# Gate and up stage in 15 pieces of 512 to 560 tokens instead of 16 of 512

## Chip, cores and metric

The kernel runs on one core of one Trainium2 chip. The metric is the device time of one execution in microseconds (us). Before the change the median of three runs is 2451.41 us (2451.37 to 2451.5).

## What is computed

`x` has shape (2, 1, 4096, 640): two sequences of 4096 tokens, 640 features each, 8192 tokens in all.

```python
g = sigmoid((x * gate_w).sum(-1, keepdims=True))
a = irfft2(mlp(rfft2(x)))        # a two-layer complex MLP in 4 blocks of 160, with ReLU and soft threshold
b = (gelu(x @ w_gate) * (x @ w_up)) @ w_down      # 640 -> 1728 -> 640
out = g * a + (1 - g) * b
```

## The kernel before

Three stages follow each other, and each fills TensorE (PE).

**Gate and up stage** (0 to about 1354 us). It makes `gelu(x @ w_gate) * (x @ w_up)`, called h, and writes it to DRAM (`hD`). The work is tiled by pieces of 512 tokens (16 of them, called tp) and by tiles of 128 of the 1728 columns (t = 0 to 13). A pair (x @ gate tile, x @ up tile) is a 2x2 block product over two halves of 256 tokens and two halves of the features, done with seven products by a scheme of sums (Strassen and Winograd): `quad` (L590). Each fp32 operand is split into a high and a low part (`high`, L285, on ScalarE, ACT; `low`, L288, on VectorE, DVE), and each product is hi·hi + hi·lo + lo·hi, so three matmuls (`prod`, L561; issued by `run`, L569, the matmul itself in L572). Weights are the stationary operand, 128 x 128; the tokens are the moving one, 256 columns. Every matmul loads its own weights.

The loop is over `keys` (L1500): group 0 has tiles 0 to 3, group 1 tiles 4 to 7, group 2 tiles 8 to 13; within a group, over the pieces. A quad is 54 matmuls. Piece 0 of group 0 goes through `plain` (L746), 60 matmuls a tile. For the pieces 3 to 12 (`FIRST`, `LAST`) of groups 0 and 1, called deep, one of the seven products is itself done by such a scheme over two pieces and two tiles: a quad is 48 matmuls there, and `deep_parts` (L692) adds 21 per two pieces and two tiles. Tile 13 is `mixed` (L772), 30 matmuls a piece in group 2.

Beside it run the first steps of the Fourier transform (`a_step`, L821): 64 rows of x, four matmuls of 320 columns each, with a stationary table `F1`, loaded on GpSimd's (POOL's) queue by `f1_load` (L791), five tables a load.

**Spectral stage** (to about 1768 us): `fwd2`, `mlp1`, `mlp2`, `inv1`. **Last stage** (to the end): `inv2` and `down` (L1402), the product with w_down, 32 steps; h is read back by `h_load` (L1318) and the split weights by `wd_load` (L1268).

The order is written out by hand: `spread` puts a step at a slot (seven slots in a quad, `hook`) of a piece, `at` after a tile, `fin` after a step of the spectral stage. `x_prep` (L468) makes the sums and splits of the next piece, or loads them from `xD` if an earlier group has made them. Each engine runs its instructions in this order, and SyncE's (SP's) queue issues most DMAs, in order too.

SBUF is divided into rings of buffers: `big` (L240) 18 buffers of 5120 bytes a partition, `mid` 14 of 4096, `small` 18, `tiny` 15. Weights take `big`, tokens (`xo`) take `mid`.

```python
def big(shape, dt=F32, name="big"):
    return pool.tile(shape, dt, name=name, tag="big", bufs=18)
```

Of the kernel before, what the change touches and what calls it, by code (L numbers as in the profile page):

```python
# [15 lines left out]
P = 128  # L16
# [10 lines left out]
FIRST, LAST = 3, 13  # L27

# [129 lines left out]

def _layouts(a):
# [10 lines left out]
    def apart(a, n):  # L170
# [51 lines left out]
def spectral_mix_kernel(ctx: ExitStack, tc: tile.TileContext, a):  # L222
# [15 lines left out]
    gap = []  # L238

    def big(shape, dt=F32, name="big"):  # L240
        return pool.tile(shape, dt, name=name, tag="big", bufs=18)

    def mid(shape, dt=F32, name="mid"):
        if not gap:
            gap.extend([tiny([P, 1], name="gap"), pool.tile([P, 112], F32, name="gap", tag="gap", bufs=1)])
            for t in gap:
                nc.gpsimd.memset(t, 0.0)
        return pool.tile(shape, dt, name=name, tag="mid", bufs=14)
# [21 lines left out]
    xD = [dram.tile([P, 4, 1024], F32, name=f"xD_{t}") for t in range(16)]  # L270
# [3 lines left out]
    xA = {t: dram.tile([P, 3584], F32, name=f"xA_{t}") for t in range(FIRST, LAST, 2)}  # L274
# [6 lines left out]
    gs = consts.tile([P, 2, 3, 32], F32, name="gs")  # L281
# [47 lines left out]
    def w_prep(t, plain=False):  # L329
# [17 lines left out]
        def st0():  # L347
            if not plain:
                gate_high()
            GR[t] = o["r"][0]  # L350
            if t < NPAIR:
                g, u = o["r"]
                x = small([P, 4, P], name="wt")
                s1, e, s4 = o["s"] = x[:, 0:2], tiny([P, 2, P], name="wt"), x[:, 2:4]
                s23 = o["s23"] = small([P, 4, P], name="wt")
                nc.vector.tensor_add(s1, u[:, 0:2], u[:, 2:4])
                nc.vector.tensor_sub(s23[:, 0:2], s1, g[:, 0:2])
# [12 lines left out]
        def st3():  # L370
            g, u = o["r"]
            e = o["s"][1]
            w2 = o["w2"] = big([P, 5, 2, P], F32R, name="w2")
            high(w2[:, 0:4, 0], o["s23"])
            nc.vector.tensor_sub(e[:, 0], u[:, 4], g[:, 4])
            nc.vector.tensor_scalar(e[:, 1], u[:, 4], -1.0, None, op0=OP.mult)

        def st4():
# [4 lines left out]
            high(w2[:, 4, 0], o["s"][1][:, 0])  # L383
            low(w2[:, 0:4, 1], o["s23"], w2[:, 0:4, 0])

        def st5():
# [4 lines left out]
            high(w1[:, 4, 0], o["s"][1][:, 1])  # L391
            low(w1[:, 0:2, 1], o["s"][0], w1[:, 0:2, 0])
            low(w2[:, 4, 1], o["s"][1][:, 0], w2[:, 4, 0])

        def st6():
# [5 lines left out]
            low(w1[:, 4, 1], o["s"][1][:, 1], w1[:, 4, 0])  # L401
# [66 lines left out]
    def x_prep(key, k, eng=nc.vector):  # L468

        name = XNAMES[k]  # L470
        kept = int(name[1]) - 1 if name in ("t1", "t2", "t3", "t4") else None

        def src():
            d = XT[key]
            if not made(key) and kept is not None:
                m = mid([P, 2, 512], F32R, name="xo")
# [3 lines left out]
            for n, p, q in (("t1", "b12", "b11"), ("t2", "b22", "t1"), ("t3", "b22", "b12"), ("t4", "b21", "t2")):  # L480
                if n not in d and (n == name or (n, name) == ("t1", "t2")):
                    d[n] = small([P, 512], name="xd")
                    nc.vector.tensor_sub(d[n], d[p], d[q])
            if name == "t5":
                d[name] = small([P, 256], name="xd")
                nc.vector.tensor_sub(d[name], d["k4"][:, :256], d["k4"][:, 256:])
            return d[name]

        def hi(copy=high):
            if not made(key) and kept is not None:  # L490
                return
            if name == "t5":
                if not T5:
                    T5.append(mid([P, 2, 2, 256], F32R, name="xo"))
                t = [T5[0][:, keys.index(key) % 2, h] for h in range(2)]
            else:
                m = mid([P, 2, 512], F32R, name="xo")
# [16 lines left out]
    def x_deep(gr, tp):  # L514
# [30 lines left out]
        def sums(k):  # L545
            def f():
                p, q = XT[0, tp]["b21"], XT[0, tp + 1]["b21"]
                a_, b_ = slice(0, 256), slice(256, 512)
                if not k:
                    x = o["x"] = [small([P, 512], name="xd") for i in range(2)]  # L550
# [25 lines left out]
    def h_store(tp, t, h):  # L576
        st(dr(hD, 4 * tp * P * 14 * P + t * P, [[14 * P, P], [P * 14 * P, 4], [1, P]]),
           h.rearrange("p (t n) -> p t n", t=4))

    def x_of(o, *names):  # L580

        tiles = []
        for n in names:
            n, q = n if isinstance(n, tuple) else (n, None)
            h, l = o[n]
            for k in ((0,) if n == "t5" else (0, 1) if q is None else (q,)):
                tiles.append((h[:, 256 * k:256 * k + 256], l[:, 256 * k:256 * k + 256]))
# [4 lines left out]
    def quad(key, t, hook):  # L592
# [3 lines left out]
        half = lambda: bank()[:, :256]  # L596
        T = lambda n: tiny([P, 256], name=n)
# [8 lines left out]
        if ahead_:  # L606
            if t % 2 == 0:
                PB[t] = big([P, 5, 256], name="pb")
            p1, u2 = (PB[t - t % 2][:, 2 * (t % 2) + k] for k in range(2))
        elif dp and t % 2 == 0:  # L610
            p1 = PB[t][:, 4]
# [17 lines left out]
        h = small([P, 512], name="h") if dp and not ahead_ else None  # L629
        if h is not None:  # L630
            u2 = h[:, :256]
# [20 lines left out]
        def half3():  # L652
            run(X, prod(w["s4"], x_of(o, "b22")), first=False)
            v["h"] = small([P, 512], name="h") if not dp else h
            v["h2"] = T("h2") if ahead_ else v["h"][:, 256:]
            gelu(v["h2"], X)

        def half4():
# [5 lines left out]
            elif not dp:  # L664
                nc.vector.tensor_mul(v["h"][:, :256], u2, p1)
# [21 lines left out]
    def half_store(tp, t, q, h):  # L687
        st(dr(hD, (4 * tp + 2 * q) * P * 14 * P + t * P, [[14 * P, P], [P * 14 * P, 2], [1, P]]),
           h.rearrange("p (t n) -> p t n", t=2))

    def deep_parts(gr, tp, t):
# [80 lines left out]
    def mixed(key):  # L772
# [3 lines left out]
        pm = bank()  # L776
        for q, (x0, x1) in enumerate((("b11", "b21"), ("b12", "b22"))):
            run(pm[:, 256 * q:256 * q + 256], prod(ws, x_of(o, x0, x1, ("k4", q))))
        s, h = small([P, 512], name="gelu"), small([P, 512], name="h")
        nc.gpsimd.memset(h[64:], 0.0)  # L780
        nc.scalar.activation(s[:64], pm[:64], AF.Gelu_apprx_tanh)
        nc.scalar.activation(h[:64], pm[64:], AF.Copy)
# [33 lines left out]
    def a_step(b, n2, h):  # L816
        xs = XS.pop((b, n2, h))
        m = n2 if n2 < 16 else 32 - n2
        f = F1[m // 5][:, m % 5]
# [13 lines left out]
    def gates(b):  # L833
        nc.scalar.activation(gs[:, b, 0], G[:, b], AF.Sigmoid)
        nc.vector.tensor_scalar(gs[:, b, 1], gs[:, b, 0], -1.0, 1.0, op0=OP.mult, op1=OP.add)
        nc.vector.tensor_scalar(gs[:, b, 2], gs[:, b, 0], -1.0, None, op0=OP.mult)
# [425 lines left out]
    def wd_load(j, part):  # L1262
# [23 lines left out]
        if part in (2, 5):  # L1286
            x = mid([P, 1024], F32R, name="wx")
            later.append(lambda: go(x[:, :960], wdf[j], 13, 10, 3))
            for k, n in enumerate(("t1", "b21", "t4")):
                put(n, 0, x[:, 320 * k:320 * k + 320])  # L1290
        elif part == 3:
            x = mid([P, 1024], F32R, name="wx")
            n = 3 if j < 6 else 1
            go(x[:, :320 * n], wdl, 7, j, n)
            for k in range(n):
                WM.setdefault(j + k, {}).setdefault("b22", [None, None])[1] = x[:, 320 * k:320 * k + 320]
            if j == 6:
# [506 lines left out]
```

## Time and profile before

| | us |
|---|---|
| median of three runs | 2451.41 |
| the profiled execution | 2451.55 |
| its span, first to last instruction | 2449.8 |
| outside the span | 1.75 |

In the span PE is busy for 2436.6 us (99%), the weight loads (PEld, beside PE) 99%, DVE 81%, ACT 62%, POOL 6%. The granted clock of PE is full in all slices. The DMA engines are busy for about 0.6 of the span.

How to read it: a matmul's record lasts longer than its share of the engine, since matmuls overlap in the pipeline (a mean of 275 ns each, 11196 of them, 1297.9 us busy together). So what a matmul costs is the distance from its start to the next one's; in a window in which PE never stops that is (length of the window + one record's duration) / matmuls counted, since the count takes in those that began just before it.

### The profile page before, as it was taken

How to read it: one execution, taken by the hardware profiler on the slowest of the kernel's cores; microseconds unless marked ns; L12 is line 12 of the kernel's file. 1: busy time of each engine (PE TensorE's matmuls, PEld its weight loads, DVE VectorE, ACT ScalarE, POOL GpSimd, SP SyncE). 2: the span in 40 equal slices, each digit the busy share in tenths (PEclk: the TensorE clock that was granted, in tenths of full speed). 3: DMA queues.
4: the chain of work that ended last, by engine and by line, in shares of the span. 5: the costliest groups of instructions: out<-in, count | busy, mean ns of one | idle time of the engine just before them, and what ended most of it. 6: DMA issues, size and time to landing. Idle time of an engine off the chain costs nothing.

```text
span 2449.8 us, 54273 instructions
## 1 busy us (share of the span) xinstructions
PE 2436.6 (99%) x20243; PEld 2428.4 (99%) x20243; DVE 1989.7 (81%) x4416; ACT 1506.8 (62%) x3565; POOL 150.2 (6%) x218
## 2 busy tenths in 40 slices
PE   9999999999999999999999999999999999999999
PEld 9999999999999999999999999999999999999999
DVE  7777787877777878777766888888898988888887
ACT  5555556666665666666555788888755555555554
POOL 0111100000000000000002211111100000000000
PEclk9999999999999999999999999999999999999999
DMA  6666667677778677777768455557864444444443
GB/s 210 209 230 217 240 208 239 213 263 240 259 231 257 206 252 253 223 246 237 234 212 260 131 160 163 161 159 235 296 211 148 151 151 168 160 162 159 155 143 105
DMA packets 351421, 499.49 MB, mean 204 GB/s; under 512 B 26028, under 2 KB 223276, under 8 KB 351156
## 3 DMA queue, kind: packets, MB, share of 16 engines
q1 hardware_dynamic: 333684, 445.02, 56.2%
q0 software_dynamic: 17472, 51.00, 5.8%
q8 instruction: 159, 2.61, 0.4%
q14 instruction: 106, 0.87, 0.1%
HBM read 307.10 MB, written 188.81 MB: 202 GB/s over the span
## 4 chain that ended last, share of the span: by engine, by line
PE 93%; DMA 2%; DVE 2%; ACT 1%; issue 1%; POOL 0%; SPq 0%; ACTq 0%; DVEq 0%; POOLq 0%
PE bank L572 73%; PE bank L307 13%; PE bank L993 3%; PE bank L704 2%; PE bank L827 1%; PE bank L1079 1%; PE bank L1080 1%; DMA xraw<-in_xT_dram 0%; DMA s<-scr 0%; DMA xo<-xD 0%; DMA scr<-is 0%; DVE w L288 0%; DMA xr<-in_x_dram 0%; DMA sc<-scr 0%; PE bank L1081 0%
## 5 line engine op out<-in xcount | busy, mean ns | idle before, releaser
L572 PE MATMUL bank<-xo,w 128*128 128x256 f32 x11196 | 1297.9, 275 | 3.9 <-DVE u L650 3.1
L572 PEld LDWEIGHTS bank<-xo,w 128*128 128x128 f32 x11196 | 1276.2, 192 | 6.4 <-DVE u L650 4.1
L572 PE MATMUL bank<-wx,ho 128*128 128x320 f32 x4608 | 631.7, 299 | 0.7 <-ACT bank L1429 0.5
L572 PEld LDWEIGHTS bank<-wx,ho 128*128 128x128 f32 x4608 | 627.7, 189 | 1.2 <-ACT bank L1429 0.8
L598 ACT ACTIVATE u<-bank 128x256 f32<-128x256 f32 x328 | 125.4, 382 | 169.8 <-PE bank L572 161.3
L288 DVE TENSOR_TENSOR ho<-hraw,ho 128x640 fp32r<-128x640 f32 (+3 forms) x384 | 194.4, 541 | 23.8 <-ACT ho L285 21.8
L285 ACT ACTIVATE ho<-hraw 128x640 fp32r<-128x640 f32 x320 | 165.9, 571 | 45.6 <-issue 39.4
L288 DVE TENSOR_TENSOR xs<-xr,xs 64x640 fp32r<-64x640 f32 x128 | 104.9, 820 | 69.8 <-ACT xs L285 67.5
L288 DVE TENSOR_TENSOR xo<-xraw,xo 128x512 fp32r<-128x512 f32 x194 | 133.1, 686 | 15.6 <-ACT xo L285 14.2
L650 DVE TENSOR_TENSOR u<-bank,u 128x256 f32<-128x256 f32 x204 | 85.7, 420 | 73.6 <-ACT u L598 72.2
L307 PE MATMUL bank<-wm,h 128*128 128x320 f32 (+1 forms) x792 | 129.7, 300 | 0.5 <-DVE h L1057 0.5
L829 DVE TENSOR_TENSOR as<-bank,as 64x320 f32<-64x320 f32 x256 | 113.7, 482 | 19.5 <-ACT as L828 17.4
L285 ACT ACTIVATE xo<-xraw 128x512 fp32r<-128x512 f32 x194 | 121.6, 627 | 6.7 <-DMA xraw<-in_xT_dram 5.5
L598 ACT ACTIVATE p<-bank 128x256 f32<-128x256 f32 x144 | 55.3, 384 | 107.0 <-DVE h L661 55.6
L307 PEld LDWEIGHTS bank<-wm,h 128*128 128x128 f32 (+1 forms) x792 | 111.8, 186 | 1.9 <-DVE h L1057 0.7
L828 ACT ACTIVATE as<-bank 64x320 f32<-64x320 f32 x256 | 96.8, 426 | 20.9 <-PE bank L827 15.8
L1429 ACT ACTIVATE bank<-bank 128x320 f32<-128x320 f32 x31 | 13.1, 422 | 156.1 <-PE bank L572 150.9
L1423 DVE SCALAR_TENSOR_TENSOR uu<-bank,gs,uu 128x320 f32<-128x320 f32 x191 | 101.8, 547 | 8.2 <-PE bank L572 4.7
L285 ACT ACTIVATE xs<-xr 64x640 fp32r<-64x640 f32 x128 | 93.8, 733 | 21.5 <-DMA xr<-in_x_dram 19.7
L599 ACT ACTIVATE h<-bank 128x256 f32<-128x256 f32 x204 | 77.9, 382 | 32.2 <-PE bank L572 30.4
L1396 DVE SCALAR_TENSOR_TENSOR uu<-bank,gs,uu 128x320 f32<-128x320 f32 x120 | 57.9, 544 | 48.7 <-ACT uu L1395 46.7
L661 DVE TENSOR_TENSOR h<-h,u 128x256 f32<-128x256 f32 x204 | 84.7, 415 | 0.0
(191 smaller groups left out, 3503.1 us busy)
## 6 DMA issues: line engine op xcount, KB each, us to landing
xo<-xD SPq DMA_DIRECT2D x124, 512.0 KB
xraw<-in_xT_dram SPq DMA_DIRECT2D x215, 256.0 KB
hD<-h SPq DMA_DIRECT2D x184, 256.0 KB
hraw<-hD SPq DMA_DIRECT2D x128, 320.0 KB
xD<-xo POOLq DMA_DIRECT2D x64, 512.0 KB, 3.3
sc<-scr SPq DMA_DIRECT2D x65, 320.0 KB
xr<-in_x_dram SPq DMA_DIRECT2D x64, 320.0 KB
scr<-as SPq DMA_DIRECT2D x64, 320.0 KB
```

Of the source, the lines that this page charges most:

```text
L285: nc.scalar.activation(dst, src, AF.Copy, scale=scale)
L288: eng.tensor_sub(dst, src, hi.bitcast(F32))
L307: nc.tensor.matmul(dst, l, by_two(r), start=i == 0, stop=i == len(ops) - 1)
L572: nc.tensor.matmul(dst, l, by_two(r), start=first and i == 0, stop=i == len(ops) - 1, skip_group_check=True)
L598: copy = lambda d, s_: nc.scalar.activation(d, s_, AF.Copy)
L599: gelu = lambda d, s_: nc.scalar.activation(d, s_, AF.Gelu_apprx_tanh)
L650: nc.vector.tensor_add(u4, C, u4)
L661: nc.vector.tensor_mul(v["h2"], v["h2"], v["u4"])
L828: nc.scalar.activation(stg[hi, cs], pa[lo, :320], AF.Copy)
L829: nc.vector.tensor_add(stg[hi, cs], pa[hi, :320], stg[hi, cs])
L993: nc.tensor.matmul(pz.rearrange("p (r e k f) -> p k r e f", r=2, e=2, k=4)[:, kp], SC[b, c, kp][:, o:o + P], ft.rearrange("p (r e f) -> p ...
L1423: nc.vector.scalar_tensor_tensor(dst, x, g, dst, op0=OP.mult, op1=OP.add)
```

## The change

The 8192 tokens are cut into 15 pieces: one of 512 (piece 0), ten of 544 (the deep ones), four of 560 (pieces 1, 2, 13, 14). A half has 256, 272 or 280 tokens, and that is the width of the moving operand.

`big` and `mid` become one ring of 29 buffers of 5120 bytes; `mid = big`. The table `F1` gets a ring of its own with a single buffer of one table; it is loaded 17 times instead of 4. h lies in DRAM as `[128, 14, 8192]` (partition, tile, token) and not by blocks of 128 tokens; a store of h is one run per partition, and a load takes seven runs of 128 tokens per partition. Several preparations stand at later slots, the sigmoid of the gate moves into the spectral stage, and the loads of w_down's weights are cut and ordered differently.

```diff
+KEYS = 15
+def half_of(t):
+    return 256 if t == 0 else 272 if FIRST <= t < LAST else 280
+def first_of(t):
+    return sum(2 * half_of(k) for k in range(t))
...
     def big(shape, dt=F32, name="big"):
-        return pool.tile(shape, dt, name=name, tag="big", bufs=18)
...
-        return pool.tile(shape, dt, name=name, tag="mid", bufs=14)
+        return pool.tile(shape, dt, name=name, tag="big", bufs=29)
+    mid = big
...
-    hD = dram.tile([64, P, 14 * P], F32, name="hD")
+    hD = dram.tile([P, 14, 2 * N], F32, name="hD")
...
     def h_store(tp, t, h):
-        st(dr(hD, 4 * tp * P * 14 * P + t * P, [[14 * P, P], [P * 14 * P, 4], [1, P]]),
-           h.rearrange("p (t n) -> p t n", t=4))
+        st(hD[:, t, first_of(tp):first_of(tp + 1)], h)
...
+        N = half_of(key[1])
-        half = lambda: bank()[:, :256]
-        T = lambda n: tiny([P, 256], name=n)
+        half = lambda: bank()[:, :N]
+        T = lambda n: tiny([P, N], name=n)
...
     def f1_load(q):
-        m = min(5, 17 - 5 * q)
-        F1[q] = big([P, 5, 2, P], F32R, name="f1")
-        nc.gpsimd.dma_start(F1[q][:, :m], a["f1"][:, 5 * q:5 * q + m])
+        F1[q] = pool.tile([P, 2, P], F32R, name="f1", tag="f1", bufs=1)
+        nc.gpsimd.dma_start(F1[q], a["f1"][:, q])
...
-        if k in (0, 18, 38, 58):
-            back(i, sp[0] - 12, lambda q=(k + 2) // 20: f1_load(q))
+        if k % 4 == 2 or not k:
+            back(i, sp[0] - (0 if k else 8), lambda q=(k + 2) // 4: f1_load(q))
...
-            for k, s in enumerate((5, 8, 11, 14, 16, 18, z + 1, z + 4, z + 6) if gr < 2 else
-                                  (6, 9, 13, 17, 21, z + 1, z + 2, z + 3, z + 3, z + 5)):
+            for k, s in enumerate(((5, 8, 11, z - 1, z + 1, 18, z + 3, z + 4, z + 6),
+                                   (5, 8, z - 3, z, z - 2, 18, z + 1, z + 5, z + 4),
+                                   (6, 9, z - 3, z + 3, z - 2, z + 1, z + 1, z + 5, z + 4, z + 6))[gr]):
...
         if part in (2, 5):
-            x = mid([P, 1024], F32R, name="wx")
-            later.append(lambda: go(x[:, :960], wdf[j], 13, 10, 3))
+            x = mid([P, 1280], F32R, name="wx")
+            def both():
+                go(x[:, 960:], wdl, 7, j, 1)
+                go(x[:, :960], wdf[j], 13, 10, 3)
+            later.append(both)
...
-    keys = [(gr, tp) for gr in range(3) for tp in ([1, 2, 0, *range(3, 16)] if gr == 1 else range(16))]
+    keys = [(gr, tp) for gr in range(3) for tp in ([1, 2, 0, *range(3, KEYS)] if gr == 1 else range(KEYS))]
```

What it moves, at three places. First PE's row in group 2, where the transform's matmuls (`xs,f`; the number belongs to the table's buffer) stand between those of the quads (`xo,w`). Before:

```order
L827 MATMUL bank<-xs,f_13809 128x320 x2
L572 MATMUL bank<-xo,w_11934 128x256 x7
L572 MATMUL bank<-xo,w_11894 128x256 x6
L572 MATMUL bank<-xo,w_11934 128x256 x9
L572 MATMUL bank<-xo,w_11740 128x256 x3
L572 MATMUL bank<-xo,w_11741 128x256 x3
L572 MATMUL bank<-xo,w_11721 128x256 x6
L572 MATMUL bank<-xo,w_12018 128x256 x9
L827 MATMUL bank<-xs,f_13809 128x320 x2
L572 MATMUL bank<-xo,w_11953 128x256 x9
```

Now:

```order
L833 MATMUL bank<-xs,f_14515 128x320 x2
L579 MATMUL bank<-xo,w_11207 128x272 x7
L579 MATMUL bank<-xo,w_11168 128x272 x6
L579 MATMUL bank<-xo,w_11207 128x272 x9
L579 MATMUL bank<-xo,w_11011 128x272 x3
L579 MATMUL bank<-xo,w_11012 128x272 x3
L579 MATMUL bank<-xo,w_10992 128x272 x6
L579 MATMUL bank<-xo,w_11291 128x272 x9
L833 MATMUL bank<-xs,f_15265 128x320 x2
L579 MATMUL bank<-xo,w_11226 128x272 x9
```

The width is 272 instead of 256; the first pair uses one table, the second another that was loaded into the same buffer, with 43 matmuls between them (7, 6, 9, 3, 3, 6 and 9).

Second, POOL's row, where the tables' loads stand (`h` is the tile that `mixed` stores). Before:

```order
L792 DMA f_9182<-in_f_dram 128x1280
L780 MEMSET h 64x512 x4
L792 DMA f_13809<-in_f_dram 128x1280
L780 MEMSET h 64x512 x7
L792 DMA f_17533<-in_f_dram 128x512
L780 MEMSET h 64x512 x2
```

Now, from the same part of group 2:

```order
L798 DMA f_13820<-in_f_dram 128x256
L784 MEMSET h 64x544
L798 DMA f_14515<-in_f_dram 128x256
L784 MEMSET h 64x544 x2
L798 DMA f_15265<-in_f_dram 128x256
L784 MEMSET h 64x544
L798 DMA f_15983<-in_f_dram 128x256
L784 MEMSET h 64x544
L798 DMA f_16687<-in_f_dram 128x256
```

A load of one table (128 x 256) stands before each table's first use, between the clearings of h.

Third, SyncE's row ahead of the last stage, behind the spectral stage's last but one store (`scr<-is`): the rest of w_down's weights (`wx`) is loaded there. Before:

```order
L264 DMA scr_1_71<-is 16x16x320 x2
L1268 DMA wx<-wdf_111 128x1280
L1268 DMA wx<-wdl 128x960 x2
L1268 DMA wx<-wdl 128x320
L1268 DMA wx<-wdf_111 128x640
L1268 DMA wx<-wdf_109 128x640
L1268 DMA wx<-wdf_110 128x640
L1268 DMA wx<-wdf_109 128x960
L1268 DMA wx<-wdf_111 128x960
L1268 DMA wx<-wdf_110 128x960
L264 DMA scr_1_71<-is 16x16x320 x2
```

Now:

```order
L270 DMA scr_1_71<-is 16x16x320 x2
L1277 DMA wx<-wdf_107 128x1280
L1277 DMA wx<-wdf_108 128x1280
L1277 DMA wx<-wdf_109 128x1280
L1277 DMA wx<-wdf_110 128x1280
L1277 DMA wx<-wdf_110 128x640
L1277 DMA wx<-wdf_108 128x640
L1277 DMA wx<-wdf_109 128x640
L1277 DMA wx<-wdl 128x320
L1277 DMA wx<-wdf_108 128x960
L1277 DMA wx<-wdl 128x320
L1277 DMA wx<-wdf_110 128x960
L1277 DMA wx<-wdl 128x320
L1277 DMA wx<-wdf_109 128x960
L270 DMA scr_1_71<-is 16x16x320 x2
```

Before, one load of 128x1280 stood behind that store; now four do, and the runs of `wdl` are single ones of 320.

## Rows read from the trace of the kernel before

**Rows 1.** The page: engine PE busy, and the granted clock in 40 slices.

```profile
PE 2436.6 (99%) x20243; PEld 2428.4 (99%) x20243; DVE 1989.7 (81%) x4416; ACT 1506.8 (62%) x3565; POOL 150.2 (6%) x218
...
PEclk9999999999999999999999999999999999999999
```

**Rows 2.** Windows, PE alone: window, length, busy (matmuls), clock, DMA share, GB/s.

```profile
150.00:250.00 100.00, 100.00 (x898) 1.00 0.67 230
...
1850.00:1950.00 100.00, 100.00 (x738) 1.00 0.50 165
```

**Rows 3.** Groups by line, PE: form xcount | busy us, mean ns | idle before.

```profile
L572 PE MATMUL bank<-xo,w 128*128 128x256 f32 x11196 | 1297.9, 275 | 3.9 <-DVE u L650 3.1 <-DVE w L288 0.5 <-ACT h L598 0.3
...
L704 PE MATMUL bank<-xo,w 128*128 128x256 f32 x240 | 39.9, 275 | 0.0
...
L704 PE MATMUL bank<-xs,w 128*128 128x256 f32 x180 | 30.1, 276 | 0.1
...
L754 PE MATMUL bank<-xo,w 128*128 128x256 f32 x60 | 8.1, 288 | 0.0
```

**Rows 4.** Timeline, weight loads (PEld), 1360.7 to 1361.9: start us, us, what, xcount.

```profile
1361.39 0.30 PEld L1012 LDWEIGHTS bank<-fny,sc 128*128 128x128 f32 x2 [0.35 <-DMA sc<-scr]
1361.61 0.41 PEld L993 LDWEIGHTS bank<-f,sc 128*128 128x128 f32 x3
```

**Rows 5.** Timeline, PE, matmuls of 258 columns in the spectral stage, 1380.4 to 1382.5.

```profile
1380.70 0.50 PE L307 MATMUL bank<-z,wm 128*128 128x258 f32 x3
...
1382.38 0.30 PE L307 MATMUL bank<-wm,h 128*128 128x320 f32 x1
```

**Rows 6.** Waits of PE, 50 to 1350: who <- for whom: us, times, longest us.

```profile
PE bank L572 <- DVE u L650: 2.5, 3, 1.2
PE bank L572 <- ACT h L598: 0.3, 1, 0.3
PE bank L827 <- DVE as L829: 0.3, 1, 0.3
```

**Rows 7.** Groups by line and form, ACT: the first halves of x.

```profile
L285 ACT ACTIVATE xo<-xraw 128x512 fp32r<-128x512 f32 x194 | 121.6, 627 | 6.7 <-DMA xraw<-in_xT_dram 5.5
...
L285 ACT ACTIVATE xo<-xd 128x512 fp32r<-128x512 f32 x69 | 43.1, 625 | 9.6 <-DVE xd L483 5.5 <-PE bank L572 4.1
```

**Rows 8.** DMA issues: out<-in engine op xcount, KB each, median us to landing.

```profile
v<-in_v_dram POOLq DMA_DIRECT2D x30, 128.0 KB, 2.3
...
f<-in_f_dram POOLq DMA_DIRECT2D x1, 256.0 KB, 2.9
```

**Rows 9.** Timeline, SyncE's queue, 1760 to 1781: start us, us, line, xcount.

```profile
1762.94 0.33 SPq L1268 DMA_DIRECT2D wx<-wdf  x1
1764.43 3.41 SPq L1268 DMA_DIRECT2D wx<-wdl  x3
1768.29 5.61 SPq L1268 DMA_DIRECT2D wx<-wdf  x6
```

**Rows 10.** Windows, PE and DMA share, 1760 to 1780.

```profile
1760.00:1770.00 10.00, 9.68 (x71) 1.00 1.03 408
1770.00:1780.00 10.00, 9.77 (x72) 1.00 1.03 411
```

**Rows 11.** Timeline, PE, 1774 to 1776.5: the third product of the last stage.

```profile
1774.07 0.30 PE L572 MATMUL bank<-wx,ho 128*128 128x320 f32 x1
1774.60 2.17 PE L572 MATMUL bank<-wx,ho 128*128 128x320 f32 x14 [0.23 <-DVE ho L288]
```

**Rows 12.** Timeline, SyncE's queue, 2000 to 2024: loads of h.

```profile
2002.65 0.38 SPq L1326 DMA_DIRECT2D hraw<-hD  x1
...
2007.54 0.37 SPq L1327 DMA_DIRECT2D hraw<-hD  x1
```

**Rows 13.** Timeline, DVE, 2000 to 2022: the first use of those loads.

```profile
2011.25 1.16 DVE L1332 TENSOR_TENSOR hraw<-hraw 128x640 f32<-128x640 f32 x2
```

**Rows 14.** Windows, all engines, last stage: PE, PEld, DVE, ACT, POOL busy (x), clock, DMA.

```profile
1800.00:2440.00 640.00, 640.00 (x4714) 640.00 (x4713) 563.42 (x1170) 337.95 (x751) 15.33 (x29) 1.00 0.46 153
```

More of the change, by code (lines that the diff above doesn't have):

```diff
@@ L352, in st0 @@
                 g, u = o["r"]
-                x = small([P, 4, P], name="wt")
-                s1, e, s4 = o["s"] = x[:, 0:2], tiny([P, 2, P], name="wt"), x[:, 2:4]
-                s23 = o["s23"] = small([P, 4, P], name="wt")
+                x, y = (small([P, 5, P], name="wt") for k in range(2))
+                s1, e, s4 = o["s"] = x[:, 0:2], (x[:, 4], y[:, 4]), x[:, 2:4]
+                s23 = o["s23"] = y[:, 0:4]
                 nc.vector.tensor_add(s1, u[:, 0:2], u[:, 2:4])
@@ L493, in hi @@
                 if not T5:
[L494 to L495 removed]
+                    T5.append(mid([P, 2, 2, 280], F32R, name="xo"))
+                t = [T5[0][:, keys.index(key) % 2, h, :N] for h in range(2)]
             else:
[L497 removed]
+                m = mid([P, 2, 2 * N], F32R, name="xo")
                 t = [m[:, h] for h in range(2)]
@@ L547, in f @@
                 p, q = XT[0, tp]["b21"], XT[0, tp + 1]["b21"]
-                a_, b_ = slice(0, 256), slice(256, 512)
+                a_, b_ = slice(0, 272), slice(272, 544)
                 if not k:
-                    x = o["x"] = [small([P, 512], name="xd") for i in range(2)]
+                    x = o["x"] = [small([P, 544], name="xd") for i in range(2)]
                     o["src"] = [p, x[0], q[:, b_], x[1][:, a_], x[1][:, b_]]
@@ L628, in quad @@
         run(X, prod(w["s2"], x_of(o, "t2", "t5")), first=False)
-        h = small([P, 512], name="h") if dp and not ahead_ else None
+        h = small([P, 2 * N], name="h") if dp and not ahead_ else None
         if h is not None:
-            u2 = h[:, :256]
+            u2 = h[:, :N]
         elif not dp:
@@ L775, in mixed @@
         ws = [(w[:, k, 0], w[:, k, 1]) for k in range(5)]
-        pm = bank()
+        N = half_of(key[1])
+        s, h = small([P, 2 * N], name="gelu"), small([P, 2 * N], name="h")
+        nc.gpsimd.memset(h[64:], 0.0)
         for q, (x0, x1) in enumerate((("b11", "b21"), ("b12", "b22"))):
[L778 to L782, printed above, removed]
+            pm, cs = bank()[:, :N], slice(N * q, N * q + N)
+            run(pm, prod(ws, x_of(o, x0, x1, ("k4", q))))
+            nc.scalar.activation(s[:64, cs], pm[:64], AF.Gelu_apprx_tanh)
+            nc.scalar.activation(h[:64, cs], pm[64:], AF.Copy)
         nc.vector.tensor_mul(h[:64], s[:64], h[:64])
@@ L833, in gates @@
     def gates(b):
-        nc.scalar.activation(gs[:, b, 0], G[:, b], AF.Sigmoid)
-        nc.vector.tensor_scalar(gs[:, b, 1], gs[:, b, 0], -1.0, 1.0, op0=OP.mult, op1=OP.add)
-        nc.vector.tensor_scalar(gs[:, b, 2], gs[:, b, 0], -1.0, None, op0=OP.mult)
+        if not spare:
+            spare.append(tiny([P, 2, 3, 32], name="gs"))
+            gs.extend(spare[0][:, k] for k in range(2))
+        nc.scalar.activation(gs[b][:, 0], G[:, b], AF.Sigmoid)
+        nc.vector.tensor_scalar(gs[b][:, 1], gs[b][:, 0], -1.0, 1.0, op0=OP.mult, op1=OP.add)
+        nc.vector.tensor_scalar(gs[b][:, 2], gs[b][:, 0], -1.0, None, op0=OP.mult)
     W1, W1L, W2, W2L = {}, {}, {}, {}
@@ L1517, in spectral_mix_kernel @@
     last = len(keys) - 1
-    at(last - 1, 1, i1_load)
+    at(last, 4, i1_load)
     at(last - 1, 3, f2_load)
     at(last - 1, 3, sc_load, *chunks[0])
-    at(last, 0, ones)
     at(last, 4, ones_h)
     at(last, 0, rest, *chunks[0])
+    at(last, 2, ones)
     at(last, 2, zl_load, *chunks[0])
@@ L1572, in spread @@
             slots.setdefault((j, q), []).append(f)
-    steps_a = [(i, j) for i in (14, *range(17, 30), *range(32, 46)) for j in ((0,) if i < 16 else (0, 1) if i < 32 else (0, 1, 2) if 32 < i < 42 else (0, 2))]
+    steps_a = [(i, j) for i in (*range(16, 28), *range(30, 44))
+               for j in ((0, 1) if i < 30 else (0, 1, 2) if 30 < i < 43 else (0, 2))]
     def back(i, s, f):
```

150 lines of the change are left out of this document (72 added, 78 removed).

## Prediction

> **What bounds the kernel now.** The page comes first: PE is busy for 2436.6 of 2449.8 us and its clock is granted in full, 2.4 GHz, in every slice [rows 1]. So the end moves only if PE's stream of matmuls gets shorter or gets holes. A busy share says nothing about how good that stream is, so the second view is the windows in which PE never pauses [rows 2]: there the length, plus the one record that reaches in from before, divided by the matmuls is the distance from one matmul's start to the next.
>
> - 256 columns, in the gate and up stage (150 to 250 us): (100 + 0.275) / 898 = 111.66 ns. 256 columns at 2.4 GHz are 106.67 ns, so 4.99 ns are on top.
> - 320 columns, in the last stage (1850 to 1950 us): (100 + 0.299) / 738 = 135.87 ns. 320 columns are 133.33 ns, so only 2.54 ns are on top.
>
> The narrower matmul costs more on top. A third view tells why: the weight loads around two matmuls of 4 columns each [rows 4]. Two loads begin at 1361.39, the next at 1361.61, so each takes its port for 0.11 us, although next to nothing streams meanwhile. Every matmul here loads its own weights. I read this as a floor: a matmul can't follow the one before by less than about 111.7 ns, the time of a weight load, however few its columns; above some 262 columns the columns set the distance, with 2.54 ns on top. 256 columns lie just under that floor, 272 and 280 above it.
>
> The waits of PE in the gate and up stage come to 3.1 us, five times in all [rows 6]: hardly anything is to be had from waits.
>
> **The matmuls.** Counted by group [rows 3]: 11196 + 240 + 180 + 60 = 11676 matmuls of 256 columns before. After, from the loops (54 a quad, 48 and a share of 21 in deep pieces, 60 in the plain ones, 300 a piece in group 2):
> - 256 columns, piece 0: 240 + 216 + 300 = 756;
> - 272 columns, the ten deep pieces: 2 x (10 x 4 x 48 + 10 x 21) + 10 x 300 = 7260;
> - 280 columns, pieces 1, 2, 13, 14: 2 x 4 x 4 x 54 + 4 x 300 = 2928.
>
> Together 10944, or 732 fewer, with almost the same columns (2,988,096 against 2,989,056). The trace has no matmul of 272 or 280 columns, so the price is bounded from both sides.
> - Floor: 272/2.4 + 2.54 = 115.87 ns, 280/2.4 + 2.54 = 119.21 ns. Before 11676 x 111.66 = 1303.7 us; after 756 x 111.66 + 7260 x 115.87 + 2928 x 119.21 = 84.4 + 841.2 + 349.0 = 1274.6 us. Gain 29.1 us.
> - Straight line between the two measured widths (0.378 ns a column): 117.71 and 120.74 ns, 84.4 + 854.6 + 353.5 = 1292.5 us. Gain 11.2 us.
> - The same 4.99 ns on top of any width in this stage: 118.32 and 121.66 ns, 84.4 + 859.0 + 356.2 = 1299.6 us. Gain 4.1 us.
>
> The nearest row, 258 columns, stands in the spectral stage [rows 5]: 15 matmuls from 1380.70 to 1382.38, 112.0 ns each. The floor asks for 1.675 us, the last model for 1.687 us; with steps of 0.01 us this doesn't decide. I take the floor, since the weight loads show it directly [rows 4] and since the 320 columns have only 2.54 ns on top.
>
> The Trainium skill, "TensorE: Matmul & The Clock Gate", section "Back-to-back issue gap", speaks against this gain: it gives an isolated gap of N/2.4 + 2.5 ns for every N at the full clock. By that rule 256 columns would take 109.2 ns and the change would save 1274.6 - 1272.4 = 2.2 us (an estimate from that page). The trace agrees at 320 columns (135.87 ns) and not at 256 (111.66 ns), and the measurement decides.
>
> **What lies beside PE.** DVE and ACT treat the same number of columns in fewer, wider instructions, and a quad gets 4% longer on PE, so both keep their cover; priced at nothing. If that cover went, the next thing late would be a bank that PE accumulates into and that ACT has to copy first (the quad's first bank, which is needed again 15 matmuls or more later, 1.7 us).
>
> **The table F1.** Reloaded 16 times into one buffer, so each reload waits for PE's last use, in POOL's queue, with the clearing of `h` queued behind it. In PE's new order the tightest pair has 43 matmuls between last and first use, 43 x 115.87 = 4.98 us. A POOL transfer lands 2.3 us after its issue at 128 KB, and 2.9 us at 256 KB [rows 8]; a table is 128 KB. 2.1 us remain. Priced at nothing; without that cover 16 x 0.6 us, about 10 us.
>
> **One ring of 29 buffers instead of 18 + 14.** Three fewer. Who waits today for a buffer that PE has to release is seen in ACT's first halves of x: 4.1 us in the stage, and none of it reaches PE [rows 7]. The new slots make x later (t3, b21 and t2 by up to 14 slots, of about 0.9 us each). Priced at nothing, bounded above in the rivals.
>
> **Ahead of the last stage.** w_down's loads are issued later, because buffers come free later. Now, behind the spectral stage's last but one store, ten are issued from 1762.94 to 1773.90 [rows 9]: 640 + 2 x 480 + 160 + 3 x 320 + 3 x 480 = 4160 KB. After, 4 x 640 + 3 x 320 + 3 x 160 + 3 x 480 = 5440 KB. The DMA engines are full there, 408 to 411 GB/s at a share of 1.03 [rows 10], so 1280 KB more cost 3.2 us of transfer. The first reader, the third product, begins at 1774.07 and today waits for DVE, not for a load [rows 11]. How long before it the loads land has no row. Bounds: 0 and 6.4 us (twice the shift, if two products are hit). I take 2 us.
>
> **Reads of h.** Each token block is read in runs of 512 bytes instead of mostly 2560. Eight loads are issued from 2002.65 to 2007.9, DVE wants the first four at 2011.25 [rows 12, 13]: more than 3.3 us after the last issue. Priced at nothing. Stores get longer runs.
>
> **The sum.** The profiled execution took 2451.55 us, its span and 1.75 us around it, 0.14 above the median shown. 2451.5 - 29.1 + 2 = 2424.4, and I say **2425 us**.
>
> **Rivals.**
> 1. *The 5 ns belong to the stage and not to the width* (operands, sequencer): with 4.1 us gained and 2 lost, 2449.4 us, no change; the rule of the skill cited above comes to the same. For it: nothing here shows a width between 258 and 320. Against: rows 4. With the straight line, 2442 us. Chance 5% for the constant, 5% for the line.
> 2. *Floor as forecast, but new holes*: x late at the start of some of the 45 - 3 = 42 runs of a group over a piece, or a longer wait ahead of the last stage, 5 to 15 us together: 2430 to 2440 us. Chance 10%.
> 3. *Slower, by the ring*: a first half of x waits on ACT for a buffer that PE still reads; the copies out of the banks stand behind it on ACT, and PE waits for those. Once in each of 42 piece runs. It decides from (29.1 - 2) / 42 = 0.65 us of hole a run; at 1 us 2451.5 - 29.1 + 2 + 42 = 2466 us. For it: three buffers fewer, and ACT's queue is strictly in order. Against: 4.1 us of such waits now, PE's holes 3.1 us. Chance 5%.
> 4. *Slower, by the reads of h*: if the runs of 512 bytes land so late that DVE, busy for 563 of 640 us in the last stage [rows 14], can't make up for it. A step is 156 matmuls (144 of the seven products, 12 of `inv2`), 21.2 us, and DVE is free for 12% of it, 2.5 us. From 3.3 + 2.5 = 5.8 us later on, each us costs 31 us; 1 us more than that gives 2456 us. Chance 3%.
>
> **Numbers.** Forecast (floor, holes of at most 4 us) 72%, rival 2 10%, rival 1 10%, rivals 3 and 4 8%. A measurement of this kernel can tell 0.2%, or 4.9 us, from no change. The range: below, 2451.5 - 29.1 - 3.1 (all waits of rows 6 gone) = 2419; above, through rival 2 to 2440. Left out are rivals 1, 3 and 4, under 2 in 10. Faster: forecast, rival 2, the line: 87%. Same: the constant and a little of rival 3: 6%. Slower: 7%.
>
> **What the new profile would show.** In a window without pauses some 115.9 ns a matmul in deep pieces and 119.2 in pieces of 560; 118.3 and 121.7 would prove rival 1. The gate and up stage should end some 29 us earlier. PE's waits there should stay under 6 us, none of them on a table; ACT's waits for PE at the halves of x tell of rival 3. Ahead of the last stage a wait of PE on `wx` of 1 to 3 us; later none. The prediction is wrong if the matmuls' distance doesn't fall per column, or if PE's waits grow by 10 us or more.

## The result, and the profile after

| | before | after |
|---|---|---|
| median | 2451.63 us (6 runs, 2451.37 to 2452.77) | 2459.62 us (6 runs, 2458.61 to 2462.66) |
| profiled execution | 2451.55 us, span 2449.8 | 2458.61 us, span 2456.8 |
| ratio | 1 | 1.0034, 95% interval 1.0021 to 1.0046 |
| PE busy | 2436.6 us, 20243 instructions | 2415.4 us, 19511 |

Slower by 0.34%, where 2425 us, faster, was forecast.

Every matmul cost what the forecast said. Windows of the changed kernel without a pause, in columns as in [rows 2] (272 columns, 280 columns, last stage):

```profile
150.00:250.00 100.00, 100.00 (x865) 1.00 0.63 230
...
60.00:80.00 20.00, 20.00 (x170) 1.00 0.48 186
...
1850.00:1950.00 100.00, 100.00 (x738) 1.00 0.54 154
```

272 columns: (100 + 0.279) / 865 = 115.93 ns (forecast 115.87); 280 columns: (20 + 0.285) / 170 = 119.3 ns (119.21); 320 columns as before. So PE's stream is shorter by the 29 us forecast, and the time went into holes. Adding up what each matmul's distance to the next exceeds its own (111.7, 115.9, 119.2 or 135.9 ns by columns) gives 23.0 us before and 59.4 us after; 36.4 - 29.4 = 7.0 us is what the span grew. By place, good to about 1 us:

| holes, us | before | after | more |
|---|---|---|---|
| at steps that use the table F1 | 0.6 | 17.9 | 17.4 |
| last 60 us of the gate and up stage | 2.6 | 16.4 | 13.8 |
| rest of that stage, start included | 9.6 | 8.2 | -1.4 |
| spectral stage | 3.3 | 5.8 | 2.5 |
| its end and the way into the last stage | 6.9 | 11.1 | 4.2 |
| last stage from there | 0.0 | 0.0 | 0.0 |

PE's waits of the changed kernel from 50 to 1357 us, beside the 3.1 us of [rows 6], name the table and two engines, ACT and DVE:

```profile
PE bank L833 <- DMA f<-in_f_dram: 14.9, 8, 5.8
PE bank L579 <- ACT u L606: 4.9, 2, 3.5
PE bank L579 <- DVE u L656: 4.6, 2, 2.6
PE bank L579 <- ACT p L606: 3.0, 2, 2.1
```

**The table.** First its row in the DMA issues of the whole changed kernel, then what was issued from 541 to 550 us, around one load that was issued at 541.71 us and landed at 549.15:

```profile
f<-in_f_dram POOLq DMA_DIRECT2D x17, 128.0 KB, 6.7
```

```profile
DMA  9999997999989999999999999998999999999999
...
q1 hardware_dynamic: 1461, 3.44, 98.9%
q0 software_dynamic: 144, 0.13, 5.6%
...
xo<-xA SPq DMA_DIRECT2D x2, 544.0 KB
xraw<-in_xT_dram SPq DMA_DIRECT2D x3, 272.0 KB
```

A table needs 6.7 us, where [rows 8] have 2.3 us for as many bytes. In those 9 us the DMA engines are full, with 3.44 MB for SyncE's queue, loads of the next piece's x above all, beside the table's 0.13 MB. In the list of packets this table's first one starts 3.7 us after the issue; for a load at 863.18 us, which landed in 3.0 us, it starts after 1.2 us. The first reload is worst, since it also stands on POOL's queue behind stores of x, which wait for DVE and ACT. POOL's timeline, 430 to 438 us, and PE's, 437 to 447:

```profile
430.42 0.53 POOL L517 DMA_DIRECT2D xD<-xo  x1 [67.11 <-DVE xo L294]
432.38 0.53 POOL L517 DMA_DIRECT2D xD<-xo  x1 [1.43 <-DVE u L656]
435.35 0.53 POOL L517 DMA_DIRECT2D xD<-xo  x1 [2.43 <-ACT h L607]
437.39 0.53 POOL L517 DMA_DIRECT2D xD<-xo  x1 [1.51 <-DVE xo L294]
437.93 0.54 POOL L798 DMA_DIRECT2D f<-in_f_dram  x1
```

```profile
437.80 2.44 PE L579 MATMUL bank<-xo,w 128*128 128x256 f32 x20
446.08 0.87 PE L833 MATMUL bank<-xs,f 128*128 128x320 f32 x2 [5.84 <-DMA f<-in_f_dram]
```

The load is issued 6.1 us after PE's last use of the old table; PE stands for 5.84 us.

**The end of the gate and up stage.** PE has four waits of over 1 us there. The first two, and what ACT, DVE and SyncE's queue did before them:

```profile
1303.21 7.41 PE L579 MATMUL bank<-xo,w 128*128 128x280 f32 x48 [2.60 <-DVE u L656]
1314.17 3.17 PE L579 MATMUL bank<-xo,w 128*128 128x280 f32 x12 [3.55 <-ACT u L606]
```

```profile
1303.24 0.96 ACT L291 ACTIVATE wf<-wx 64x320 fp32r<-64x320 f32 x2 [4.22 <-DMA hD<-h]
...
1312.17 0.96 ACT L291 ACTIVATE wf<-draw 64x320 fp32r<-64x320 f32 x2 [4.67 <-DMA wdf<-wf]
...
1313.73 0.39 ACT L606 ACTIVATE u<-bank 128x280 f32<-128x280 f32 x1
```

```profile
1302.35 0.45 DVE L493 TENSOR_TENSOR xd<-xraw 128x280 f32<-128x280 f32 x1 [4.24 <-DMA wdf<-wf]
1302.72 0.44 DVE L656 TENSOR_TENSOR u<-bank,u 128x280 f32<-128x280 f32 x1
```

```profile
1295.52 0.32 SPq L270 DMA_DIRECT2D wdf<-wf  x1
1296.60 0.32 SPq L270 DMA_DIRECT2D hD<-h  x1
...
1304.81 0.38 SPq L270 DMA_DIRECT2D wdf<-wf  x1
```

ACT and DVE want a buffer of the `small` ring (18 of 2560 bytes), for `wf`, a split piece of w_down, and for `xd`, a difference of two halves of x. The one they are given still holds an `h` or a `wf` whose store is under way, and behind `wf` and `xd` stand the copies and sums `u` that PE needs. The three stores land 6.6 to 7.3 us after their issue; from 1296 to 1313 us the DMA engines are busy for 0.96 of the time.

The other two, 1.35 and 1.99 us, end on no store:

```profile
1349.61 0.98 PE L579 MATMUL bank<-xo,w 128*128 128x280 f32 x6 [1.35 <-ACT u L606]
1352.59 1.67 PE L579 MATMUL bank<-xo,w 128*128 128x280 f32 x11 [1.99 <-DVE u L656]
```

```profile
1342.64 3.08 DVE L932 SCALAR_TENSOR_TENSOR wl<-bh,sgn,rs 2x640 fp32r<-2x640 f32 x1 [3.18 <-POOL wl L923]
```

```profile
ACT bh L291 <- DVE rs L910: 3.1, 1, 3.1
```

Here the spectral stage's weights are prepared: DVE waits for POOL, ACT for DVE, and PE for both. The kernel before has no such wait of ACT at its `bh`; the changed kernel and each of its variants below has it, with both holes in PE's stream. With a stretch at half the clock behind them they make some 5 of the 16.4 us; the small ring makes some 11.

**The clock.** PE's granted clock falls in or right behind such holes. In the kernel before it is 1.00 from the first matmul to the last, and the 40 slices of the page are too coarse to show the change. Windows in and behind the first one, and one at the end of the stage:

```profile
442.60:449.40 6.80, 3.32 (x14) 0.50 0.18 61
449.50:456.30 6.80, 6.80 (x63) 1.00 0.20 54
```

```profile
1313.00:1319.80 6.80, 5.63 (x25) 0.50 0.39 136
```

There are five stretches at 0.50 (1.2 GHz) of 3.4 or 6.8 us, 23.9 us in all, and the matmuls in them account for 8.5 of the 59.4 us.

### The profile page after: what moved, and what is told of

The parts are those of the page before. It is cut to its first block, busy times and chain, and to the rows that moved or that the text cites. A ratio compares the mean times of both kernels' runs of the same rounds, so it can differ in the third digit from the quotient of the medians.

```text
span 2456.8 us, 52653 instructions
## 1 busy us (share of the span) xinstructions
PE 2415.4 (98%) x19511; PEld 2406.6 (98%) x19511; DVE 1984.8 (81%) x4323; ACT 1493.6 (61%) x3507; POOL 156.3 (6%) x224
## 4 chain that ended last, share of the span: by engine, by line
PE 51%; DMA 4%; issue 4%; DVE 2%; ACT 2%; POOL 0%; SPq 0%; ACTq 0%; POOLq 0%; DVEq 0%
PE bank L579 35%; PE bank L313 12%; PE bank L1002 2%; DMA f<-in_f_dram 1%; DMA scr<-as 1%; DMA sc<-scr 1%; DMA wdf<-wf 1%; PE bank L1088 0%; PE bank L1089 0%; DMA wx<-wdl 0%; PE bank L833 0%; DMA wx<-wdf 0%; DMA zl<-zl 0%; PE bank L1090 0%; DMA scr<-is 0%
## 5 line engine op out<-in xcount | busy, mean ns | idle before, releaser
L579 PE MATMUL bank<-xo,w 128*128 128x272 f32 (+2 forms) x10464 | 1270.8, 281 | 13.6 <-ACT u L606 4.9
L579 PEld LDWEIGHTS bank<-xo,w 128*128 128x128 f32 x10464 | 1247.2, 190 | 15.2 <-ACT u L606 5.3
L606 ACT ACTIVATE u<-bank 128x272 f32<-128x272 f32 (+2 forms) x302 | 119.6, 396 | 159.1 <-PE bank L579 151.6
L291 ACT ACTIVATE ho<-hraw 128x640 fp32r<-128x640 f32 x320 | 168.9, 571 | 39.0 <-PE bank L579 30.4
L656 DVE TENSOR_TENSOR u<-bank,u 128x272 f32<-128x272 f32 (+2 forms) x191 | 84.1, 440 | 86.0 <-ACT u L606 85.4
L606 ACT ACTIVATE p<-bank 128x272 f32<-128x272 f32 (+2 forms) x151 | 60.1, 398 | 138.2 <-PE bank L579 74.8
L294 DVE TENSOR_TENSOR xo<-xraw,xo 128x544 fp32r<-128x544 f32 (+2 forms) x181 | 130.4, 720 | 5.2 <-ACT xo L291 3.8
L291 ACT ACTIVATE xo<-xraw 128x544 fp32r<-128x544 f32 (+2 forms) x181 | 118.1, 652 | 5.0 <-DMA xraw<-in_xT_dram 3.8
L607 ACT ACTIVATE h<-bank 128x272 f32<-128x272 f32 (+2 forms) x191 | 75.5, 395 | 33.7 <-PE bank L579 33.2
L1002 PE MATMUL bank<-f,sc 128*128 128x128 f32 x640 | 84.5, 279 | 0.7 <-DMA sc<-scr 0.7
```

The costliest lines, as they stand in the source:

```text
L291: nc.scalar.activation(dst, src, AF.Copy, scale=scale)
L294: eng.tensor_sub(dst, src, hi.bitcast(F32))
L579: nc.tensor.matmul(dst, l, by_two(r), start=first and i == 0, stop=i == len(ops) - 1, skip_group_check=True)
L606: copy = lambda d, s_: nc.scalar.activation(d, s_, AF.Copy)
L607: gelu = lambda d, s_: nc.scalar.activation(d, s_, AF.Gelu_apprx_tanh)
L656: nc.vector.tensor_add(u4, C, u4)
```

## The experiments

In the program's order, each write into a small buffer can be given a distance: the matmuls between the issue of the store that it waits for and the write. The closest in the changed kernel are 12, 20, 25, 25, 29 and 30 matmuls, some 1.4 to 3.5 us; in the kernel before, 61 in this stage. (These come from the order in which the program is built; the trace has no buffer numbers.) What the trace has is the landing: in the changed kernel the stores for which ACT or DVE waited over 0.5 us landed 6.6 to 9.3 us after their issue, not the 3 to 5 us that the expectation of e6 takes. The runs of the kernel before beside these experiments had medians of 2450.99, 2451.57 and 2452.6 us.

**e1, the floor alone.** In the quads of the kernel before:

```diff
+        def run(dst, ops, first=True):
+            for i, (l, r) in enumerate(ops):
+                n = 256 if first and i == 0 else 240
+                nc.tensor.matmul(dst[:, :n], l, by_two(r[:, :n]), start=first and i == 0, stop=i == len(ops) - 1,
+                                 skip_group_check=True)
...
```

> The kernel before, with every matmul of the quads but the first of each accumulation cut from 256 to 240 columns (10,004 of them; it leaves out the last 16 columns of each half, so its output is incomplete). Theory 'floor' (a matmul of these sizes costs the load of its own weight, about 0.11 us): pitch stays at 111.7 ns and the time at 2451 us, within 3. Rival 'so many ns a column plus a constant': 10,004 x 6.67 = 67 us less, 2385 us. Rival 'straight line from 256 to 320 columns' (0.378 ns a column): 10,004 x 6.05 = 61 us less, 2391 us.

Measured: 2469.19 us, ratio 1.0075 (1.0059 to 1.009). Its window from 150 to 250 us has as many matmuls as with 256 columns [rows 2]:

```profile
150.00:250.00 100.00, 100.00 (x898) 1.00 0.67 231
```

111.66 ns for 240 columns: the floor holds, and both rivals fall. The Trainium skill, "TensorE: Matmul & The Clock Gate", section "Back-to-back issue gap", gives by its formula an isolated gap of 102.5 ns for 240 columns, and says itself that in a stream with weight loads both set the distance; the measurement decides, and it is 111.7. But the time rose by 18 us, where none was expected, and not one instruction had moved on any engine. PE's holes come to 38.0 us instead of 23.0; ACT's timeline shows one of the new waits:

```profile
944.14 0.76 ACT L836 ACTIVATE as<-bank 64x320 f32<-64x320 f32 x2
950.24 0.38 ACT L607 ACTIVATE h<-bank 128x256 f32<-128x256 f32 x1 [5.34 <-DMA scr<-as]
```

In the kernel before the same `h` (939.55 us) follows `as` without a pause: ACT waits here, 5.34 us, for a store that it did not wait for before. My reading is that the tiles got other ones of the 18 buffers when the program was built with other matmul sizes (closest distance 37 instead of 61); the trace shows the waits, not the buffers.

**e2, no reloads.** All A steps use the first table:

```diff
-        f = F1[m]
+        f = F1[0]
...
-        if k % 4 == 2 or not k:
+        if not k:
```

> The changed kernel, with the table F1 loaded once and never again: all 64 A steps use the first of the 17 tables (it leaves out the other 16, so the A steps' results are not the reference's). Theory 'tables' (16 reloads into the only buffer land 3 to 8 us after their issue and TensorE waits): the 14.9 us of waits for f<-in_f and the slow clock after the first go, 17 us less than the changed kernel, 2442 us (2439 to 2446). Rival 'the cost is in the ring of small buffers alone, and a wait removed here is waited elsewhere': 2456 to 2460 us.

Measured: 2444.23 us, 15.4 less than the changed kernel. The tables cost what they seemed to, less 2 us: with PE no longer standing there, four waits for ACT's `p` stand at 927, 1001, 1075 and 1150 us where there were two, 5.3 us instead of 3.0.

**e3, w_down's rounds earlier.** 60 slots apart instead of 65, begun 5 slots sooner.

> The changed kernel, with the preparation of the down weights (seven rounds) spaced 60 slots instead of 65 and begun 5 slots earlier, so that it ends 35 slots before the gate stage's end. Theory 'crowded end' (in the last two pieces ACT and DVE wait for small buffers that are still being stored, TensorE stands, and its clock is halved after that): most of the 18.7 us of holes between 1300 and 1357 us go, 2445 us (2440 to 2450). Rival 'crossings' (any round of weight splits that meets the stores of an A step costs 1 to 2 us; moving them makes as many new ones): 2455 to 2462 us. Rival 'the end waits for something else' (loads for the next stage): unchanged, 2459.

Measured: 2454.64 us (11 runs, 2449.73 to 2460.35), 5 less: the end is better, but the closest distances were only 25 to 38 matmuls, and holes of 1.5 to 2.2 us came in the middle of the stage (the rival "crossings").

**e4, tables in a large buffer**, five to a load, as before.

> The changed kernel, with the table F1 five at a time in a large buffer and four loads, as in the kernel before (it takes one of the 29 large buffers). Theory 'tables': as with one table never reloaded, 2442 us (2439 to 2446). Rival 'ring of large buffers' (29 are just enough; one less makes the splits of activations wait): 2450 us or more, with new waits of ACT for a large buffer. If the ring of small buffers meets the A steps at other moments, some us either way.

Measured: 2499.12 us, the opposite of what I expected. The rival's time came, but not its waits of ACT for a large buffer. ACT's waits from 900 to 1357 us, those for DMAs among the first eight:

```profile
ACT wf L291 <- DMA scr<-as: 23.9, 4, 7.0
...
ACT xs L291 <- DMA xr<-in_x_dram: 13.2, 7, 4.5
ACT wf L291 <- DMA hD<-h: 11.4, 3, 7.4
```

The first and the last are small buffers again, given out otherwise (closest distances 12, 13, 16, 20, 21, 21); the one between them is a late load of x. Whether the 29 large buffers could spare one is not told by this run.

**e5, the table in two halves.** A half's buffer is free after its own last use; no byte more of memory:

```diff
-        F1[q] = pool.tile([P, 2, P], F32R, name="f1", tag="f1", bufs=1)
-        nc.gpsimd.dma_start(F1[q], a["f1"][:, q])
+        q, h = q
+        F1[q, h] = pool.tile([P, P], F32R, name="f1", tag=f"f1{h}", bufs=1)
+        nc.gpsimd.dma_start(F1[q, h], a["f1"][:, q, h])
...
+        if k % 4 == 1 and k < 62:
+            for h in range(2):
+                back(i, sp[3 + h] + 1, lambda q=(k // 4 + 1, h): f1_load(q))
```

> The changed kernel, with the table's buffer (1024 B) in two halves of 512 B, one for each half of an A step: a half is loaded again one slot after its own last use, so it has 10 to 13 slots (some 70 to 110 matmuls, 8 to 12 us) until its next use instead of 6 to 10. Nothing else moves. Theory 'tables': loads of 6 to 8 us fit in, the 15 us of waits for f<-in_f go, and with them the slow clock after 446 us: 2443 to 2446 us, as with one table never reloaded (2444.2). Rival 'a load lands when the next burst of loads of x is through, whenever it was issued': half the waits stay, 2451 us. Rival 'a POOL that waits for TensorE a second time per table delays the stores and memsets behind it': no gain, 2458 us.

Measured: 2445.88 us, ratio to the kernel before 0.9975 (0.9966 to 0.9984). The loads are no quicker, but no longer waited for: their row, and PE's only wait for them.

```profile
f<-in_f_dram POOLq DMA_DIRECT2D x34, 64.0 KB, 5.8
```

```profile
PE bank L833 <- DMA f<-in_f_dram: 0.5, 2, 0.3
```

Half the bytes take 5.8 us instead of 6.7, so the size is the smaller part of it. The first reload also moved: it is issued at 433.03 us, ahead of two of the four stores of x on POOL's queue and not behind them. So the gain is that of more cover and of this place together.

**e6, one slot.** The rounds 64 slots apart instead of 65:

```diff
-        spread(i, 65 * j, p0)
+        spread(i, 64 * j, p0)
```

and so for the two lines behind it.

> The changed kernel, with the seven rounds of preparing the down weights 64 slots apart instead of 65, begun at the same slot. In the program's order, ACT's or DVE's first write of a small buffer then stands 33 and 37 matmuls behind the store that it waits for at the two closest places, where it is 12, 20, 25, 25, 29 and 30 at the six closest now (61 in the kernel before). Theory 'small ring': a store needs 3 to 5 us from issue to landing, 25 to 40 matmuls, so the waits of ACT and DVE for hD, wdf and scr shrink to almost nothing, the 18.7 us of holes at 1300 to 1357 us shrink to under 5 and those of 2.2 and 1 us at 1163 and 1013 go: 2444 us (2440 to 2448). Rival 'crossings move': e3 took 5 us off where its closest five were 25 to 38; by that 2453 us. Rival 'the end is crowded whatever the spacing' (loads, ACT's own work): 2456 us or more.

Measured: 2448.76 us (2444.77 to 2451.59), 10.9 less. That is just above the 2440 to 2448 us of the theory, below the 2453 us of its rival. The holes of the last 60 us fall from 16.4 to 8.1 us, and not to under 5, since those at the spectral stage's weights stay; those at the tables hardly change. Of ACT's waits for stores at the end one of 4.3 us is left, though the closest distance is 33 now:

```profile
ACT wf L291 <- DMA wdf<-wf: 4.3, 1, 4.3
```

**e7, e5 and e6 together.**

> Both edits together: the table in halves, and the rounds 64 slots apart. If tables and small ring are the two causes and apart from each other, their gains add: 2430 us (2426 to 2434), faster than the kernel before by 0.8%. Rival 'what one gives the other takes' (PE that no longer stands meets the stores earlier): 2438 us or more. TensorE's clock stays at 1.0 through the gate stage under the first.

Measured: **2429.21 us, ratio 0.9907 (0.9892 to 0.9922)**. This beats both kernels. It gains 30.4 us on the changed kernel where e5 and e6 have 13.7 + 10.9 = 24.6; the new waits for ACT's `p` that e2 and e5 showed are gone too. PE's waits from 50 to 1357 us, all of them:

```profile
PE bank L579 <- ACT u L606: 3.5, 2, 2.1
PE bank L579 <- DVE u L656: 2.0, 1, 2.0
PE bank L833 <- ACT as L834: 1.2, 3, 0.7
PE bank L1021 <- DMA sc<-scr: 0.2, 1, 0.2
```

The holes come to 31.6 us; one stretch of 3.4 us at half the clock is left in the stage, which was not expected. It lies behind the holes at the spectral stage's weights, 1.5 and 2.15 us at 1322 and 1325 us.

**e8, 63 slots.** As e7, with 63 for 64 and each round's sums two slots sooner.

> As with both edits (table in halves, spacing of the rounds), but 63 slots apart instead of 64, and each round's sums two slots earlier. In the program's order the closest small buffer that is written while its store may be under way now stands 30 matmuls behind that store, near 1000 us (with 64: 33 and 37, both in the last two pieces). Theory 'small ring': the hole of 2.3 us at 1285 us (ACT waiting for wdf and hD) goes, one of under 1 us comes near 1000 us: 2427 to 2428 us against 2429.2. Rival 'the holes at the end come from the preparation of the next stage's weights (DVE, POOL and ACT waiting for one another), whatever the spacing': 2429 to 2430 us.

Measured: 2429.25 us, as e7 and as the rival had it. The hole at 1285 us went, as the theory had it, but the spectral stage's end took the gain (13.3 us of holes there, 11.0 in e7). Of the two holes at the spectral stage's weights the rival is right: they stayed, at 1319 and 1322 us.

**e9, stores sooner.** In the changed kernel:

```diff
         hook(6)
+        flush()
         v = {}
```

> The changed kernel with one line more: the stores that have gathered are issued in the middle of each quad too, not only at its end (some 3 us sooner for half of them). Spacing 65 and the table's single buffer stay. If what ACT and DVE wait for is the stores, it gains without moving any round: the closest distances are 12, 30, 39 and 40 matmuls instead of 12, 20, 25, 25, 29 and 30: 2453 us (2449 to 2456), the table's waits staying at 15 us. Rival 'SP, which now waits for DVE's results in the middle of a quad, holds back the loads of x behind it': 2460 us or more. Rival 'the waits are for something else that the spacing changed': 2459 us.

Measured: 2485.37 us, the rival "SP holds back the loads". My edit also did other than I wrote: `hook(6)` is the end of `quad`, so the stores are hardly sooner, but they now stand on SyncE's queue ahead of the loads of x that are issued after the quad, and no longer behind them. From 79 us of the changed kernel to 326 us each load of x from `in_xT` is issued 43 to 66 matmuls later in PE's stream than without the edit. ACT waits for one until 172 us, and PE for ACT, there and four times more:

```profile
ACT xo L291 <- DMA xraw<-in_xT_dram: 5.3, 1, 5.3
```

```profile
PE bank L579 <- ACT h L606: 10.4, 5, 2.9
```

The first 400 us have some 24 us of holes instead of 4, the last 60 us about as many as without the edit (before 1340 us ACT waits 11.2 us for one store of `wf`). So a store put on SyncE's queue before its data is ready held back the loads behind it; whether stores that really come sooner would help was not tried.

## Why the prediction was wrong

1. **The matmuls: right.** 115.9 and 119.3 ns measured, some 29 us of PE's stream gone, and the floor shown directly by e1.
2. **"The table F1 ... 2.1 us remain. Priced at nothing": the step that failed.** The cover of the tightest reload, 43 matmuls or 4.98 us, was as computed; three of the 16 have it, five have 61 matmuls. The transfer was not: 6.7 us in the median, and not the 2.3 or 2.9 us of [rows 8]. The 2.3 us belong to the last stage, where the DMA engines are busy for about half the time [rows 14]. The 2.9 us, from which the 2.1 us were worked out, are a single load of this table, 256 KB at 1156 us in the gate and up stage. The page of the kernel before had the three others from that stage too, five tables at a time:

```profile
f<-in_f_dram POOLq DMA_DIRECT2D x3, 640.0 KB, 6.6
```

   Taken as the bound from above, it would have given 16 x (6.6 - 5.0), 26 us, enough to eat the gain; measured 17.4 us, from eight reloads that PE waited for and the slow clock behind the first. The price "without that cover", 16 x 0.6 us, rests on no row: a reload without cover costs its whole transfer, 16 x 2.3 = 37 us even by [rows 8]. And POOL's queue was passed over: the stores of x ahead of the first reload cost 6.1 us of its cover.
3. **The ring that was priced was the wrong one.** "Three fewer. Priced at nothing" is right for the large buffers. Of the 4.1 us for which ACT's first halves of x waited for PE [rows 7], made from `xd`, none is left at any form made from `xd`, and 0.3 us stand at one made from `xraw`:

```profile
L291 ACT ACTIVATE xo<-xd 128x544 fp32r<-128x544 f32 x45 | 29.2, 649 | 2.6 <-DVE xo L294 1.9 <-DMA xD<-xo 0.6
L291 ACT ACTIVATE xo<-xraw 128x560 fp32r<-128x560 f32 x52 | 34.5, 664 | 4.3 <-DMA xraw<-in_xT_dram 3.8 <-PE bank L579 0.3
```

   But the change moved A steps, w_down's rounds and the sums against each other, and all these share the 18 small buffers, whose stores land slowly at the same moments. No term and no rival had that; it makes some 11 of the 16.4 us of holes in the last 60 us of the stage. e6 shows how little it hangs on: one slot. The other 5 us, the preparation of the spectral stage's weights on POOL, DVE and ACT, had no term either ("DVE and ACT ... keep their cover; priced at nothing").
4. **"Ahead of the last stage ... I take 2 us": right in kind.** PE waits 1.7 us for `wx`:

```profile
PE bank L579 <- DMA wx<-wdl: 1.7, 2, 1.2
```

   with 1.4 us on DVE's `h` and a stretch at half the clock the place lost 4.2 us more than before.
5. **"Reads of h ... Priced at nothing": right.** From 1800 to 2440 us PE has no pause, with the same matmuls as [rows 14] and a DMA share of 0.55 instead of 0.46:

```profile
1800.00:2440.00 640.00, 640.00 (x4714) 640.00 (x4714) 564.33 (x1171) 339.47 (x753) 15.38 (x29) 1.00 0.55 156
```

6. **The rivals.** None came as written. The second ("floor, but new holes", 5 to 15 us) is nearest in kind, with other causes and 36.4 us. The third and the fourth, the ways I saw to a slower kernel, did not happen. The prediction's own sign of being wrong did: PE's waits in the stage grew from 3.1 to 27.4 us.
7. **What a hole costs** was counted once; where the clock is halved behind it, the matmuls there add 8.5 us in all.

e2, e5 and e7 show the table's part, e6 and e7 the part of the small buffers. No run took away the holes at the spectral stage's weights, and none had more than 18 small buffers, which would test that ring directly. That the landing times come from full DMA engines is read from the trace and was not tried by itself (a load kept clear of the loads of x).

## What to carry to other kernels

Take a transfer's time from the stage in which it will run, and from its long rows there: not from a row of the same size elsewhere, and not from the shortest of four. List what stands ahead of it on its queue. Where steps are moved against each other, go through every ring of buffers that they share, with the distance from a store's issue to the next write of its buffer, and hold it against the landing times of stores in that stretch. Here stores took 6.6 to 9.3 us: at 33 and 37 matmuls (4 us) ACT still waited 4.3 us (e6), at 61 or more once 1.4 us (the kernel before). An edit that moves nothing can bring such waits (e1). When PE is bound, a gain on its stream is safe only if everything that it waits for keeps its lead.

## What the hardware showed that was not expected

- 240 and 256 columns cost the same 111.66 ns; 272 and 280 cost 2.6 ns more than their columns.
- A hole of PE can be paid twice: after 5.84 us without a matmul at 446 us the granted clock was 0.50 for 6.8 us; after the two of 1.5 and 2.15 us in e7 it was 0.50 for 3.4 us. The size of a hole alone does not tell it: after one of 2.3 us (e7, 1285 us) and one of 2.6 us (changed kernel, 1222 us) the clock stayed at 1.00; after one of 2.1 us (e6, 1218 us) and one of 1.8 us (e1, 1024 us) it was 0.50 for 3.4 us.
- A load of 128 KB landed in 3.0 to 8.0 us in this stage. More than half of what is added lies ahead of its first packet (3.7 us against 1.2). The DMA share does not tell it by itself: the load at 1064.72 us took 6.7 us at a share of 0.81, the one of 256 KB at 1156 us in the kernel before 2.9 us at 0.83. The Trainium skill, "DMA: Bandwidth & Descriptors", section "Queues, rings and completion order", says that a DMA engine takes turns between the queues that have work, a packet at a time. By that one would expect a short transfer to be through early beside a long one, which the page does not say itself; the trace fits it only behind the first packet, where the 128 rows took 3.1 us amid the burst and 1.5 us without it.
